# Loads, products and stores of three side jobs cut into quarters and moved to other steps of a two-branch attention kernel

## The chip, the cores and the metric

The kernel runs on one core of a Trainium2 chip. Its engines are TensorE (PE; its weight loads are listed apart as PEld), VectorE (DVE), ScalarE (ACT), GpSimd (POOL) and SyncE (SP), which here only issues DMA transfers. The metric is the device time of one execution in microseconds, lower is better. Three executions of the kernel before gave 2044.47, 2052.12 and 2060.83 us; the time before is their median, 2052.12.

## The reference

Two attention branches over the same input of 2048 tokens and 512 features, with 32 heads of width 16, mixed by a gate per token:

```
qkv = (x @ wqkv)                                  # branch A: softmax attention over all 2048 keys
p = softmax(q k^T * scale);  a = (p v) @ wo

for s in range(4):                                # branch B: four segments of 512 tokens
    p = softmax(qs ks^T * scale + mask); a_dot = p vs        # attention within the segment
    a_mem = (phi(qs) M) / (phi(qs) z + 1e-6)                 # read the memory
    o = g * a_mem + (1 - g) * a_dot
    M, z = M + phi(ks)^T vs, z + sum(phi(ks))                # write the memory
b = o @ wo
out = sigmoid(x . gate_w) * a + (1 - sigmoid(x . gate_w)) * b
```

All matrices are float32. The kernel splits an operand into a high and a low part of the fast matmul type where it needs the accuracy.

## The kernel before

**Stages.** First (0 to about 340 us) projections: queries, keys and values of both branches are computed and put into DRAM, with the memory's numerators (`numd`) and denominators (`dend`) for segments c = 1 to 3. Then comes one long loop over steps, and at the end the last output tiles.

**Steps.** The list `steps` (lines 103 to 109) has two parts. Branch A has 8 groups of 4 heads, each with 4 chunks of 512 queries; such a unit (group, chunk) has 16 steps, one for each block of 128 keys, so 512 steps (`nA`). Branch B has 32 units of 4 steps. In step t, `score_parts` (line 579) computes scores with the keys on the partitions, ACT turns them into p (line 582), in B POOL masks p (line 584), and `values` (line 601) multiplies p of an earlier step with the values, 17 rows for each head, the 17th being the sum of p.

**The rows of maxima.** The score matmuls use 50 rows: 48 of query parts and 2 rows with the negative maximum of each query, so that the exponent is safe. These maxima are computed 22 steps ahead of the scores in A (`max_parts`, matmul at line 197, DVE reduction at line 199). After a unit's last part `finish_max` (lines 158 to 170) reduces on DVE (line 162) and casts on POOL (lines 168, 169); 3 steps later `transpose_max` transposes on PE (line 175), copies on ACT (line 177), and sends two DMA transfers of 8 KB into rows 48 and 49 of the query tile (line 179, `qA<-mt`). In A this is recorded at the end of step 12 of every 16, and the scores of the unit it belongs to begin at step 0 of the next 16.

**Order.** The order is written by hand: `at(t, f)` records work that is issued at the start of step t (`beside`), ahead of the step's own matmuls; the rows of maxima are recorded at its end (`run_late`). Each engine and the SP queue work through their own instructions in this order, and wait for what each instruction needs. SP is not tied to the steps of the other engines: it issues the next transfer as soon as its own waits are met. Each transfer has one of eight semaphores in turn, so it also waits for the transfer that had the same one before.

**The side jobs.** Three of them are touched by the change:
- *Octets.* When the two groups of an octet of 8 heads are done, `a_invert_load` brings the sums of p, `recip` and `invert` make the reciprocal times the gate and store it (`rdA`, line 632), `a_load` (lines 651 to 653) loads the outputs of all 2048 queries and the inverse, broadcast over 16 rows, 1 MB each; `a_mul` scales a quarter on POOL (line 656), and `a_store` (line 658) puts it into DRAM in four transfers. For octet o this begins at t0 = 128 (o + 1) + 4; the load is at t0 + 8, the products at t0 + 13 to t0 + 19, the stores at t0 + 21. Octet 3 falls into branch B.
- *The memory's part.* The same for the numerators of segment c (`m_invert_load` to `m_store`, lines 663 to 679), from t0 = 24 c on: 1 MB of numerators in one transfer, the inverse in four of 256 KB, four products on POOL (line 676), one store of 1 MB.
- *Values.* `load_v` (lines 549 to 557) loads the values of a group of A in four transfers of 136 KB, all at step 64 g - 12.

Other transfers that stand in the same queue are those of the queries (`load_q`, lines 137, 138), the keys (`load_k`, lines 146, 147) and the attention outputs (line 611). POOL also splits the output weights (lines 541, 542), at steps 45 to 51 and 75 to 81.

## Time and profile before

| | us |
|---|---|
| runs (median) | 2044.47, 2052.12, 2060.83 (2052.12) |
| the profiled execution | 2040.8, span 2039.1 |
| PE busy | 2001.6 (98% of the span) |
| DVE busy | 1688.3 (83%) |
| ACT busy | 1478.2 (72%) |
| POOL busy | 212.0 (10%) |
| mean granted TensorE clock | 0.953 |

A page of the profile shows one execution. Busy time is the time in which an engine works on an instruction; a busy PE is not a PE at its peak, since its matmuls overlap. The granted clock is the share of full speed that TensorE is given. "SPq" is the queue of transfers that SP issues: the length of such a line is the time of issuing, not that of moving the data. In a line of the timeline the bracket at its end has the idle time before it and who ended it. The stages by time: projections to about 340 us, branch A's steps from there to about 1590 us, branch B's to about 1965 us, the last output tiles to 2039 us.

### The profile page before, as it was taken

The numbers are of one execution on the slowest core, as the hardware profiler recorded it, in microseconds if no ns is written. First come the engines' busy times: TensorE is split into PE (matmuls) and PEld (weight loads), VectorE is DVE, ScalarE is ACT, GpSimd is POOL, SyncE is SP. The second block draws the span as 40 slices with busy tenths as digits, with TensorE's granted clock in tenths as the row PEclk, the third lists the DMA queues.
The fourth block names the chain that finished last, engine by engine and source line by source line (L and its number), as shares of the span: only waits on it lengthen the run. The fifth ranks groups of instructions, "written<-read, shape, count | busy, mean of one in ns | idle before, by whom it ended". The sixth has DMA issues, their size and how long they took to land.

```text
span 2039.1 us, 41498 instructions
## 1 busy us (share of the span) xinstructions
PE 2001.6 (98%) x16113; PEld 912.9 (45%) x16113; DVE 1688.3 (83%) x3476; ACT 1478.2 (72%) x2823; POOL 212.0 (10%) x372
## 2 busy tenths in 40 slices
PE   8999999999999999999999999999999999999998
PEld 6887665333333333333333333333333344454545
DVE  3235896999999899999999999999998567787842
ACT  3234334888888788888888888888888855565652
POOL 3000000021200100000010000010000023343330
PEclk9999999999999899999999999999999955698989
DMA  6667434032400410110221111130103144546542
GB/s 225 216 232 241 166 141 150 31 100 94 138 15 26 93 44 26 38 35 26 59 66 39 30 30 38 32 94 15 38 15 75 54 121 138 150 146 180 163 132 91
DMA packets 94725, 190.69 MB, mean 94 GB/s; under 512 B 15888, under 2 KB 30000, under 8 KB 91712
## 3 DMA queue, kind: packets, MB, share of 16 engines
q1 hardware_dynamic: 93536, 187.30, 30.6%
q8 instruction: 127, 2.08, 0.4%
q0 software_dynamic: 992, 0.74, 0.2%
q14 instruction: 70, 0.57, 0.1%
HBM read 111.94 MB, written 74.86 MB: 92 GB/s over the span
## 4 chain that ended last, share of the span: by engine, by line
PE 86%; DVE 5%; DMA 4%; ACT 3%; issue 1%; SPq 1%; DVEq 0%; ACTq 0%
PE st L579 35%; PE ops L601 31%; PE pr L274 12%; PE fin L747 4%; DVE pm L199 3%; PE sm L197 2%; ACT p L582 2%; PE sm L210 2%; DMA qA<-mt 1%; ACT oraw L608 1%; DVE sm L215 1%; PE num L422 1%; DMA inv<-rdB 1%; PE mt_ps L175 1%; SPq L694 0%
## 5 line engine op out<-in xcount | busy, mean ns | idle before, releaser
L582 ACT ACTIVATE p<-st 128x512 f32<-128x512 f32 (+2 forms) x2432 | 1298.2, 585 | 301.0 <-PE sm L210 120.8
L199 DVE TENSOR_REDUCE pm<-sm 128x1 f32<-128x512 f32 x2048 | 1254.5, 684 | 31.2 <-PE sm L197 25.1
L579 PE MATMUL st<-qA,k 50*128 50x512 f32 x2048 | 751.4, 447 | 7.7 <-DMA qA<-mt 4.8
L197 PE MATMUL sm<-k,qA 48*128 48x512 f32 x2048 | 751.6, 451 | 0.7 <-DVE pm L199 0.5
L601 PE MATMUL ops<-p,vA 128*17 128x256 f32 x8176 | 645.5, 388 | 5.7 <-ACT oraw L608 5.6
L579 PEld LDWEIGHTS st<-qA,k 50*128 50x128 f32 x2048 | 303.4, 185 | 433.2 <-ACT p L582 411.2
L215 DVE CUSTOM_DVE_ANT_0 sm<-sm,cmask 128x256 f32<-128x256 f32 (+3 forms) x512 | 244.0, 512 | 104.7 <-PE sm L210 81.4
L197 PEld LDWEIGHTS sm<-k,qA 48*128 48x128 f32 x2048 | 310.6, 185 | 24.9 <-DVE pm L199 12.4
L601 PEld LDWEIGHTS ops<-p,vA 128*17 128x17 f32 x8176 | 135.7, 95 | 367.6 <-issue 347.4
L210 PE MATMUL sm<-k,qB 48*128 48x256 f32 (+3 forms) x512 | 183.7, 446 | 5.3 <-DVE pm L215 2.8
L579 PE MATMUL st<-qB,k 50*128 50x256 f32 (+3 forms) x512 | 174.0, 441 | 0.8 <-ACT p L582 0.2
L579 PEld LDWEIGHTS st<-qB,k 50*128 50x128 f32 x512 | 100.4, 235 | 133.5 <-issue 63.1
L168 POOL CAST ms<-nm 128x16 fp32r<-128x16 f32 x64 | 14.1, 220 | 1200.3 <-DVE nm L162 1150.0
L601 PE MATMUL ops<-p,vB 128*17 128x512 f32 (+3 forms) x1024 | 121.6, 556 | 0.0
L323 DVE TENSOR_TENSOR q<-pr,q 128x512 fp32r<-128x512 f32 x64 | 44.0, 687 | 88.0 <-ACT q L316 84.7
L210 PEld LDWEIGHTS sm<-k,qB 48*128 48x128 f32 x512 | 101.8, 233 | 14.7 <-DVE pm L215 9.8
L584 POOL TENSOR_SCALAR_AFFINE_SELECT p<-p 128x512 f32<-128x512 f32 x128 | 82.8, 647 | 244.2 <-ACT p L582 244.2
L316 ACT CAST q<-pr 128x512 fp32r<-128x512 f32 x64 | 37.4, 585 | 82.8 <-PE pr L274 65.6
L215 DVE DVE_READ_ACCUMULATOR2_ANT pm<- 128x1 f32 x512 | 72.2, 141 | 0.1
L274 PE MATMUL pr<-xh,wql 128*128 128x512 f32 x128 | 55.5, 434 | 8.0 <-ACT xh L367 6.0
L274 PE MATMUL pr<-xl,wqh 128*128 128x512 f32 x128 | 51.5, 402 | 0.0
L274 PE MATMUL pr<-xh,wqh 128*128 128x512 f32 x128 | 51.2, 400 | 0.0
(137 smaller groups left out, 1258.4 us busy)
## 6 DMA issues: line engine op xcount, KB each, us to landing
qdA<-q SPq DMA_DIRECT2D x32, 256.0 KB
kdA<-q SPq DMA_DIRECT2D x32, 256.0 KB
qdB<-q SPq DMA_DIRECT2D x32, 256.0 KB
k<-kdA SPq DMA_DIRECT2D x64, 128.0 KB
kdB<-q SPq DMA_DIRECT2D x32, 256.0 KB
qA<-qdA SPq DMA_DIRECT2D x64, 128.0 KB
odA<-oraw SPq DMA_DIRECT2D x32, 256.0 KB
k<-kdB SPq DMA_DIRECT2D x64, 128.0 KB
```

The lines of the kernel that those rows point to most:

```text
L197: nc.tensor.matmul(ps, rows(q[:, :, s * 128:(s + 1) * 128], h, 48), rows(kt_[side, g, kc], h, 48), start=True, stop=True)
L199: nc.vector.tensor_reduce(pm[:, h, s, kc:kc + 1], ps, axis=AX.X, op=ALU.max)
L210: nc.tensor.matmul(ps[:, n0:n0 + n], rows(q[:, :, s * 128:(s + 1) * 128], h, 48), rows(kt_[side, g, c][:, :, :n], h, 48), start=True, stop ...
L215: nc.vector.tensor_tensor_reduce(r, r, cmask[:, CH - n:], 1.0, -3.0e38, ALU.add, ALU.max, pm[:, h - per + 1 + e, s, 0:1])
L274: nc.tensor.matmul(ps, l(a, k), r(b, k), start=(n == 0), stop=(n == 11))
L316: nc.scalar.copy(q1, ps)
L323: nc.vector.tensor_sub(q2, ps, q1.bitcast(F32))
L579: nc.tensor.matmul(ps[:, h % per, :n], rows(k[:, :, b * 128:(b + 1) * 128], h, 50), rows(q[:, :, q0:], h, 50), start=True, stop=True)
L582: nc.scalar.activation(p[:, h - per + 1:h + 1, :n], ps[:, :, :n], AF.Exp, scale=SCALE)
L584: nc.gpsimd.affine_select(out=p[:, :, 0:128], in_=p[:, :, 0:128], pattern=[[0, 4], [1, 128]], base=0, channel_multiplier=-1, compare_op=AL ...
L601: nc.tensor.matmul(ops[32 * h:32 * h + 17, q0 + a:q0 + b], v[h], p[:, h, a:b], start=(i == 0 and a == 0), stop=(i == last and b == n), til ...
L747: nc.tensor.matmul(ps, l[:, o], r[:, o], start=(n == 0), stop=(n == 23))
```

## The change

The three side jobs are cut into quarters, each with its own load, product and store. A new helper, `apart(t, n)`, picks n steps from t on that are at least 3 apart and whose number modulo 16 is 0 to 8 or 14. A quarter's product is recorded 4 steps after its load, its store 6 steps after it. For octet 3 the quarters are 2 steps apart instead.

```diff
-    def load_v(side, i):
+    def load_v(side, i, c=0):
         if side == "A":
-            t = va.tile([128, 4, 4, 68], F32, tag="v", name=f"vA{i}")
-            for c in range(NCH):
-                nc.sync.dma_start(t[:, c], vdA[c][i])
+            t = vt[side, i] if c else va.tile([128, 4, 4, 68], F32, tag="v", name=f"vA{i}")
+            nc.sync.dma_start(t[:, c], vdA[c][i])
...
-    def a_load(o):
-        nc.sync.dma_start(big(("Ar", o), "raw"), odA[o][:, 0:16].rearrange("h r t -> r h t"))
-        nc.sync.dma_start(big(("Ai", o), "inv"), heads(rdA[o], S))
+    def a_load(o, c):
+        if c == 0:
+            big(("Ar", o), "raw")
+            big(("Ai", o), "inv")
+        ts = slice(c * CH, c * CH + CH)
+        nc.sync.dma_start(held["Ar", o][:, c], odA[o][:, 0:16, ts].rearrange("h r t -> r h t"))
+        nc.sync.dma_start(held["Ai", o][:, c], heads(rdA[o][:, ts], CH))
...
-    def a_store(o):
-        for c in range(NCH):
-            nc.sync.dma_start(atd[c][:, o], held["Ar", o][:, c])
+    def a_store(o, c):
+        nc.sync.dma_start(atd[c][:, o], held["Ar", o][:, c])
...
-    def m_load(c):
-        nc.sync.dma_start(big(("Mr", c), "am"), numd[c])
-        t = big(("Mi", c), "at")
-        for o in range(NO):
-            nc.sync.dma_start(t[:, o], heads(rdM[c][8 * o:8 * o + 8], CH))
+    def m_load(c, o):
+        if o == 0:
+            big(("Mr", c), "am")
+            big(("Mi", c), "at")
+        nc.sync.dma_start(held["Mr", c][:, o], numd[c][:, o])
+        nc.sync.dma_start(held["Mi", c][:, o], heads(rdM[c][8 * o:8 * o + 8], CH))
...
-    def m_store(c):
-        nc.sync.dma_start(amd[c], held["Mr", c])
+    def m_store(c, o):
+        nc.sync.dma_start(amd[c][:, o], held["Mr", c][:, o])
...
+    def apart(t, n):
+
+        r = []
+        while len(r) < n:
+            if t % 16 in (0, 1, 2, 3, 4, 5, 6, 7, 8, 14):
+                r.append(t)
+                t += 3
+            else:
+                t += 1
+        return r
+
     for g in range(NG):
-        at(max(0, g * 64 - 12), lambda g=g: load_v("A", g))
+        for c in range(NCH):
+            at(max(0, g * 64 - 18 + 2 * c), lambda g=g, c=c: load_v("A", g, c))
...
-        at(t0 + 7, lambda c=c: m_load(c))
-        for o in range(NO):
-            at(t0 + 10 + 2 * o, lambda c=c, o=o: m_mul(c, o))
-        at(t0 + 18, lambda c=c: m_store(c))
+        for o, n in enumerate(apart(t0 + 8, NO)):
+            at(n, lambda c=c, o=o: m_load(c, o))
+            at(n + 4, lambda c=c, o=o: m_mul(c, o))
+            at(n + 6, lambda c=c, o=o: m_store(c, o))
...
-        at(t0 + 8, lambda o=o: a_load(o))
-        for c in range(NCH):
-            at(t0 + 13 + 2 * c, lambda o=o, c=c: a_mul(o, c))
-        at(t0 + 21, lambda o=o: a_store(o))
+        for c, n in enumerate(apart(t0 + 9, NCH) if o < NO - 1 else range(t0 + 9, t0 + 9 + 2 * NCH, 2)):
+            at(n, lambda o=o, c=c: a_load(o, c))
+            at(n + 4, lambda o=o, c=c: a_mul(o, c))
+            at(n + 6, lambda o=o, c=c: a_store(o, c))
```

For octets 0 to 2 the loads so come at t0 + 10, 13, 16 and 19 (steps 142, 145, 148 and 151 for octet 0), the products at 146, 149, 152 and 155, the stores at 148, 151, 154 and 157. For the memory's part the loads are at steps 32, 35, 38, 46 (c = 1), 56, 62, 65, 68 (c = 2) and 80, 83, 86, 94 (c = 3). The values of group g come at 64 g - 18, - 16, - 14 and - 12. The values of branch B are loaded as before.

## The prediction

> **What bounds the kernel now.** I read the waits first, then the DMA queue's timeline around the longest of them, the engines' timeline there, and the windows of 10 us. The wait that carries this case is one line: engine, who waited for what, us in total, times, longest.

> ```profile
> PE st L579 <- DMA qA<-mt: 4.8, 3, 2.0
> ```

> TensorE waits three times for a row of maxima, the 16 KB that line 179 sends into the query tile. Over the page's 40 slices of 51 us one slice of the long stage shows it: DVE and the granted clock fall together in the 14th.

> ```profile
> DVE  3235896999999899999999999999998567787842
> ...
> PEclk9999999999999899999999999999999955698989
> ```

> From 350 to 1590 us (attention over all keys, 512 steps in 32 units of 16) PE and DVE are both busy 98 to 100%, so what stops PE there is lost for good. In the B stage after it, DVE is 5 to 9 tenths busy and the clock wanders between 0.50 and 1.00. The timeline of the DMA queue (start, length of the issue) shows the cause of the first wait:

> ```profile
> 651.91 1.28 SPq L179 DMA_DIRECT2D qA<-mt  x2
> ...
> 687.97 0.34 SPq L632 DMA_DIRECT2D rdA<-rec  x1
> 688.35 0.59 SPq L652 DMA_DIRECT2D raw<-odA  x1
> 689.52 0.54 SPq L653 DMA_DIRECT2D inv<-rdA  x1
> 692.59 1.41 SPq L179 DMA_DIRECT2D qA<-mt  x2
> 694.10 0.34 SPq L146 DMA_DIRECT2D k<-kdA  x1
> ...
> 738.44 1.30 SPq L179 DMA_DIRECT2D qA<-mt  x2
> 778.07 1.28 SPq L179 DMA_DIRECT2D qA<-mt  x2
> ```

> Two loads of 1 MB (L652, L653) go out 3 to 4 us ahead of the row. At the 210 GB/s of the window 690 to 700, 2.1 MB take 10 us, to about 698.5, and the chain of waits has the row landing 8.87 us after its issue. Its first reader should have run at 699.6:

> ```profile
> 701.59 0.46 PE L579 MATMUL st<-qA,k 50*128 50x512 f32 x1 [2.00 <-DMA qA<-mt]
> ...
> 702.60 4.96 POOL L656 TENSOR_TENSOR raw<-raw,inv 128x512 f32<-128x512 f32 x4 [17.21 <-DMA inv<-rdA]
> ...
> 702.81 0.79 PE L579 MATMUL st<-qA,k 50*128 50x512 f32 x1
> ```

> After the gap the same matmul takes 0.79 us where it took 0.50. Windows (PE, PEld, DVE, ACT, POOL busy; then clock, DMA share, GB/s):

> ```profile
> 690.00:700.00 10.00, 9.59 (x97) 3.32 (x93) 9.96 (x17) 8.83 (x17) 0.00 (x0) 1.00 0.96 210
> 700.00:710.00 10.00, 8.41 (x52) 2.93 (x52) 5.31 (x9) 4.93 (x9) 4.96 (x4) 0.64 0.19 32
> 710.00:720.00 10.00, 10.00 (x88) 3.26 (x84) 8.71 (x15) 7.66 (x15) 0.00 (x0) 0.85 0.73 210
> ...
> 1020.00:1030.00 10.00, 8.85 (x94) 3.10 (x86) 8.88 (x16) 7.85 (x16) 4.99 (x4) 1.00 0.54 110
> 1340.00:1350.00 10.00, 8.37 (x86) 2.96 (x84) 8.40 (x15) 7.42 (x14) 4.99 (x4) 1.00 0.48 98
> ```

> Only the first gap cost clock; the second and third (waits of 1.15 and 1.63 us) stayed at 1.00.

> **The change, part by part.** The price of each stall is read from the distance between two rows of maxima. Undisturbed it is 39.63 us (778.07 - 738.44). The three units after a load of an octet take 45.85, 40.85 (from 1016.92 to 1057.77) and 41.34 us (from 1336.27 to 1377.61): 6.22 + 1.22 + 1.71 = 9.15 us over. The units before them take 40.68, but that 1.05 is the reciprocals (four of 0.34 and a product of 0.29 on a full DVE), which stay.

> *Octets 0 to 2.* The row is queued at the end of the octet's step t0 + 8 (step 140 for octet 0). The old loads are recorded at the start of that step, ahead of it; the first new quarter comes at step 142, behind it. SP runs ahead of the steps as far as its waits let it, so quarter 0 (2 x 256 KB), the 384 KB of a key tile and quarter 1 will leave together right behind the row, some 1.4 MB; only quarters 2 and 3 are held, by the attention output's wait for ACT (L611) and the stores' wait for POOL. What counts is therefore the place behind the row, not the three steps between. Removed: 9.15 us.

> The next row (step 156) has the store of quarter 2 ahead of it in the queue. That store waits for its product, recorded at step 152, ahead of the cast of the maxima (step 153) on POOL. Quarter 2 is issued behind L611, 12.7 us after the row (664.61 after 651.91), and before the cast some 20 us remain; 2 MB took at most 14.3 us from issue to product (688.35 to 702.60). Cost 0; without that cover the cast itself would be late, and with it the row. The store of quarter 3 is behind the row.

> *Octet 3 (B stage).* Loads at 525, 527, 529, 531 instead of all at 524; the products keep steps 529 to 535 among POOL's masks of p, which the values' matmuls wait for. The 2 MB filled the DMA from 1660 to 1670 (share 1.01), yet the units around it take 12.34 and 12.33 us with or without: nothing to gain. Quarter 3 now waits for the store of quarter 0 and thus for a product: issue about 1681, 11 us before its product began (1692.14). A quarter needs 2.5 us at 210 GB/s plus a fixed part that I bound between 1.55 us (a landing of 64 KB, rdM<-rec) and 5.7 us (inv<-rdB in the chain). 4 to 8 us: cost 0.

> *The memory's part.* Chunks c = 1 to 3, loads of 256 KB and four stores in place of one. Rows in this stretch are 39.9 to 40.5 us apart, 2.57 us over in total, where three sets of reciprocals at 1.05 would give 3.15: no stall to remove. Stores of quarters 1 and 2 of c = 1 come ahead of the row of step 44; their products wait only for POOL's cast at 445.1, so they leave by about 447, five us before that row (452.03). Two products fall among POOL's splits of the output weights (0.61 + 1.28 us each), with over 25 us to the next cast. Cost 0, at most one late row: 1.2 to 6.2 us.

> *Values.* The same 32 loads of 136 KB; two of each four now leave right behind a row, two stay behind L611. No wait for them is in the list. 0.

> *Issue.* Octets gain 4 x 6 loads, the memory's part 3 x 3 loads and 3 x 3 stores: 42 issues of 0.34 to 0.6 us, some 19 us of a queue that waits 645.7 us for rows of maxima alone. 0.

> [...]

> Sum: 9.15 us less. The profiled execution took 2040.8 (span 2039.1), so it would take 2031.7. The median shown is 2052.12, 11.3 above it; the same saving from the median gives **2043.0**.

> **The rivals.**
> *Only the waits come back.* The gap and the fall of the clock may be neighbours rather than cause and effect: then 2.00 + 1.15 + 1.63 = 4.8 us return and the other 4.4 us stay, 2047.3. Against it: the clock fell within 1.3 us after the gap and nowhere else between 350 and 1620. For it: two like gaps cost none.
> [...]

> *The clock falls at all three gaps in the runs that set the median.* 3 x 6.22 = 18.7 us, 2033.5. For it: the profiled run is 11.3 below the median, and two more falls of some 4.5 each are 9.

> *A row is held up by what follows it too.* 1.4 MB right behind it instead of 2 MB ahead; if the transfers share the engines rather than follow one another, the row is late as before: no gain, 2052. Against: at 694.10 and in every fourth unit 384 KB follow a row at once, and from 612 us on no unit without an octet is longer than 39.65.

> *Slower: the half clock in B lasts longer.* Everything after 1580 shifts by 9 us, and B stands at the edge: half clock from 1626 to 1720, 0.84 to 1750, 1.00 from 1780. Units take 12.33 us at half clock against 10.35, 9.89 and 10.20 at 0.84; with output products 13.8 against 11.4 (mean of the five from 1785.20 to 1842.15). If it stayed half until 1842: 3 x 2.2 + 5 x 2.4 = 18.6 us more, net 9.4 slower, 2061.5. It decides from some 40 us of 0.84 clock lost on. For it: the runs differ by 16 us without any change. Against: nothing in the change makes PE wait there.

> **How the numbers follow.** Forecast 0.56; only the waits 0.12; three falls 0.10; no gain 0.10; half clock 0.12. The range: the forecast less the 7.7 by which the lowest run lies under the median, and on to the three falls with some of the same, 2031; above, past no gain and into the half clock, 2056. What a measurement of this kernel can tell from no change is about 1%, 20.5 us. Faster by that, under 2031.6, is the lower part of the three falls and the tail of the forecast: 0.13. Over 2072.6 is only the worst of the half clock: 0.07. Same: 0.80.

> **What would show it.** Rows of maxima 39.6 us apart in the units after octets 0 to 2 (40.7 in those with reciprocals), no line "PE st <- DMA qA<-mt", clock 1.00 from 700 to 720, loads of an octet issued behind the row. Wrong would be: a row still landing over 7 us after its issue, POOL's cast of the maxima behind a product that waits for its quarter, or B longer than its old 458 us (1581 to 2039) by more than 9.

## The result and the profile after

| | before | after |
|---|---|---|
| first comparison, median (range, runs) | 2050.55 (2044.47 to 2060.83, 4) | 2027.20 (2026.33 to 2030.35, 4) |
| profiled execution (span) | 2040.8 (2039.1) | 2026.4 (2024.7) |
| mean granted clock | 0.953 | 0.96 |

The ratio of after to before is 0.9884, with a 95% interval of 0.9842 to 0.9926. Two later comparisons, with 12 runs of the changed kernel each, give 0.9937 (0.9911 to 0.9963) and 0.9931 (0.9904 to 0.9957): 0.6 to 0.7% faster, some 13 to 14 us. The first comparison flatters the change, since its four runs of the kernel before were high: their median is 2050.55, and the later batches have 2042.30 to 2046.91.

In the list of waits of the changed kernel no line has a score matmul waiting for `qA<-mt`. The 14th slice of the page, where DVE and the granted clock both had an 8, is filled. (The clock's 8 in the 7th slice is the half clock up to 354 us; it lies ahead of the stretch that the change works on.)

```profile
DVE  4235886999999999999999999999998576687842
...
PEclk9999998999999999999999999999999965599999
```

The timeline of the DMA queue (start, length of the issue, line, transfer) shows the row of maxima of 694.67 with octet 0's loads (now L655, L656) behind it:

```profile
690.06 0.34 SPq L631 DMA_DIRECT2D rdA<-rec  x1
694.67 1.32 SPq L179 DMA_DIRECT2D qA<-mt  x2
696.04 0.57 SPq L655 DMA_DIRECT2D raw<-odA  x1
696.72 0.57 SPq L656 DMA_DIRECT2D inv<-rdA  x1
697.38 0.53 SPq L146 DMA_DIRECT2D k<-kdA  x1
...
699.35 0.52 SPq L655 DMA_DIRECT2D raw<-odA  x1
699.91 0.60 SPq L656 DMA_DIRECT2D inv<-rdA  x1
707.37 0.34 SPq L610 DMA_DIRECT2D odA<-oraw  x1
...
708.25 0.53 SPq L655 DMA_DIRECT2D raw<-odA  x1
...
712.27 0.54 SPq L655 DMA_DIRECT2D raw<-odA  x1
...
734.30 1.41 SPq L179 DMA_DIRECT2D qA<-mt  x2
735.81 0.35 SPq L662 DMA_DIRECT2D atd<-raw  x1
```

Quarter 0, the key tile and quarter 1 go out within 6 us of the row; quarter 2 waits until the attention output of 707.37 has been issued. The next row, 734.30, comes 39.63 us after this one. The windows at the places of the three old gaps (busy time of PE, PEld, DVE, ACT, POOL with counts; clock, DMA share, GB/s) are full, and the clock stays at 1.00:

```profile
700.00:710.00 10.00, 9.81 (x100) 3.44 (x96) 9.80 (x17) 9.05 (x18) 2.57 (x2) 1.00 0.61 132
710.00:720.00 10.00, 10.00 (x104) 3.44 (x96) 10.00 (x17) 8.93 (x18) 1.28 (x1) 1.00 0.92 238
1020.00:1030.00 10.00, 9.81 (x98) 3.43 (x97) 9.80 (x17) 9.05 (x18) 1.56 (x2) 1.00 0.49 150
1340.00:1350.00 10.00, 9.81 (x104) 3.44 (x96) 9.80 (x17) 9.05 (x18) 1.29 (x1) 1.00 0.57 135
```

POOL's timeline shows that the products (L659) leave the cast of the next maxima (L168) alone: quarter 2 is done by 715.10, and the cast comes at 727.35 as soon as DVE has finished; the fourth product stands right behind it.

```profile
713.82 1.28 POOL L659 TENSOR_TENSOR raw<-raw,inv 128x512 f32<-128x512 f32 x1 [6.95 <-DMA inv<-rdA]
727.35 0.20 POOL L168 CAST ms<-nm 128x16 fp32r<-128x16 f32 x1 [12.25 <-DVE nm L162]
...
727.81 1.28 POOL L659 TENSOR_TENSOR raw<-raw,inv 128x512 f32<-128x512 f32 x1
```

To see where time goes, I cut each profiled span at two places of the DMA queue: the first row of branch A after 350 us and the last one. "A" is the stretch between them, "rest" what follows (branch A's last 50 us or so, branch B and the end; branch A's last scores come at 1621 us in the kernel before, not at the 1590 of the stages by time). Between the profiles of before and after A went from 1198.80 to 1189.55, 9.25 us less; rest from 468.4 to 461.1, 7.3 less; and the projections ahead of A took 2.1 more. So of the 14.4 us between the two spans only 9.25 stand where the change works.

### The profile page after: what moved, and what is told of

It reads as the page before. It is cut to its first block, busy times and chain, and to the rows that moved or that the text cites. A ratio compares the mean times of both kernels' runs of the same rounds, so it can differ in the third digit from the quotient of the medians.

```text
span 2024.7 us, 41583 instructions
## 1 busy us (share of the span) xinstructions
PE 1991.4 (98%) x16113; PEld 909.2 (45%) x16113; DVE 1687.3 (83%) x3476; ACT 1478.6 (73%) x2823; POOL 212.9 (11%) x372
## 4 chain that ended last, share of the span: by engine, by line
PE 88%; DVE 4%; ACT 3%; DMA 3%; issue 1%; SPq 1%; POOL 0%; DVEq 0%; ACTq 0%
PE st L578 36%; PE ops L600 32%; PE pr L274 11%; PE fin L750 4%; PE sm L197 2%; PE sm L210 2%; ACT p L581 2%; DVE pm L199 1%; ACT oraw L607 1%; DMA raw<-xT 1%; DVE sm L215 1%; PE num L422 1%; PE mt_ps L175 1%; DMA at<-atd 1%; DMA k<-kdB 0%
## 5 line engine op out<-in xcount | busy, mean ns | idle before, releaser
L168 POOL CAST ms<-nm 128x16 fp32r<-128x16 f32 x64 | 14.1, 220 | 1112.6 <-DVE nm L162 1062.3
L600 PE MATMUL ops<-p,vB 128*17 128x512 f32 (+3 forms) x1024 | 117.1, 538 | 0.3 <-ACT oraw L607 0.3
```

The lines of the kernel that those rows point to most:

```text
L600: nc.tensor.matmul(ops[32 * h:32 * h + 17, q0 + a:q0 + b], v[h], p[:, h, a:b], start=(i == 0 and a == 0), stop=(i == last and b == n), til ...
```

## The experiments

Each batch of kernels ran on one chip beside runs of the kernel before. This table gathers what was read from their profiles. The waits are those of PE for the row. An octet's unit means here the one after its loads.

| kernel | A, us | waits after octets 0, 1, 2 | rest, us | ratio to before (95%) |
|---|---|---|---|---|
| before | 1198.80 | 2.00, 1.15, 1.63 | 468.4 | |
| before_again | 1205.10 | 0.95, 2.34, 2.26 | 465.5 | 1.0020 (0.9993 to 1.0047) |
| rest_only | 1200.78 | 1.42, 1.89, 2.27 | 466.1 | 1.0009 (0.9986 to 1.0031) |
| three_ahead | 1220.14 | 5.79, 6.50, 6.39 | 469.0 | 1.0102 (1.0042 to 1.0162) |
| quarters_ahead | 1201.19 | 0.58, 1.28, 1.29 | 458.1 | 0.9931 (0.9902 to 0.9960) |
| quarters_again | 1197.06 | none, 1.50, 1.73 | 465.3 | 0.9957 (0.9934 to 0.9980) |
| after | 1189.55 | none | 461.1 | 0.9884 (0.9842 to 0.9926) |
| after_again | 1189.59 | none | 470.3 | 0.9937 (0.9911 to 0.9963) |
| after_third | 1189.48 | none | 462.1 | 0.9931 (0.9904 to 0.9957) |
| octets_only | 1189.58 | none | 476.5 | 0.9936 (0.9905 to 0.9968) |
| whole_behind | 1189.57 | none | 464.2 | 0.9950 (0.9924 to 0.9976) |
| half_ahead | 1189.34 | none | 464.8 | 0.9941 (0.9908 to 0.9974) |
| octet3_whole | 1189.62 | none | 468.0 | 0.9936 (0.9913 to 0.9960) |
| recip_one | 1188.18 | none | 460.4 | 0.9922 (0.9890 to 0.9954) |

**The kernel before, once more (before_again).** The same kernel, profiled a second time.

> The kernel before, unchanged, for a second profile and for its spread. Theory one (the surplus of the saving over 9.15 us comes from the clock falling at more of the three gaps than in the first profile): two or three of the units after octets 0 to 2 are longer than 45 us, and the part of the loop over all keys is 4 to 9 us longer than the first profile's 1198.80 us between its first and last row of maxima. Theory two (it comes from stage B): those units again take 45.9, 40.9 and 41.3 us, and the rest of the execution after the last row of branch A takes more than the first profile's 468.4 us.

The median was 2048.14 of 12 runs (2030.6 to 2056.5), against 2042.57 of the 30 runs of the kernel before on that chip (2030.58 to 2056.15). The profile has the three waits again, with other lengths and other consequences. Its three first readers, from PE's timeline (in the bracket the idle time before), and the windows behind the second and third:

```profile
704.69 0.47 PE L579 MATMUL st<-qA,k 50*128 50x512 f32 x1 [0.95 <-DMA qA<-mt]
...
1025.20 0.46 PE L579 MATMUL st<-qA,k 50*128 50x512 f32 x1 [2.34 <-DMA qA<-mt]
...
1351.22 0.74 PE L579 MATMUL st<-qA,k 50*128 50x512 f32 x1 [2.26 <-DMA qA<-mt]
```

```profile
700.00:710.00 10.00, 9.05 (x92) 3.33 (x88) 9.09 (x16) 8.05 (x16) 3.84 (x4) 1.00 0.53 110
1020.00:1030.00 10.00, 7.66 (x68) 2.43 (x60) 7.00 (x12) 6.16 (x12) 4.98 (x4) 0.85 0.55 104
1030.00:1040.00 10.00, 10.00 (x60) 3.19 (x60) 5.77 (x10) 5.33 (x11) 0.00 (x0) 0.50 0.54 181
1350.00:1360.00 10.00, 8.78 (x50) 2.89 (x52) 5.16 (x8) 4.45 (x9) 4.97 (x4) 0.56 0.09 16
```

Here the first gap left the clock at 1.00, and after the second and third it was halved: after the second, PE ran a whole window at 0.50, with 60 matmuls where a full one has about 100. The three units were 40.64, 47.62 and 46.10 us long, 15.5 us over instead of 9.2. This is the first of the two theories: two units over 45 us and A 6.3 us longer. The rest, 465.5 us, is no longer than the first profile's 468.4, as the second would have it. The saving that the change can bring thus differs from execution to execution; the last section has what was measured of the falls.

**The parts by themselves (octets_only, rest_only).** One kernel has only the octets' part of the change, the other only the memory's part and the values:

```diff
# octets_only, against the changed kernel
...
-            at(max(0, g * 64 - 18 + 2 * c), lambda g=g, c=c: load_v("A", g, c))
+            at(max(0, g * 64 - 12), lambda g=g, c=c: load_v("A", g, c))
...
-        for o, n in enumerate(apart(t0 + 8, NO)):
-            at(n, lambda c=c, o=o: m_load(c, o))
-            at(n + 4, lambda c=c, o=o: m_mul(c, o))
-            at(n + 6, lambda c=c, o=o: m_store(c, o))
+        at(t0 + 7, lambda c=c: m_load(c))
+        for o in range(NO):
+            at(t0 + 10 + 2 * o, lambda c=c, o=o: m_mul(c, o))
+        at(t0 + 18, lambda c=c: m_store(c))
# rest_only, against the changed kernel
...
-        for c, n in enumerate(apart(t0 + 9, NCH) if o < NO - 1 else range(t0 + 9, t0 + 9 + 2 * NCH, 2)):
-            at(n, lambda o=o, c=c: a_load(o, c))
-            at(n + 4, lambda o=o, c=c: a_mul(o, c))
-            at(n + 6, lambda o=o, c=c: a_store(o, c))
+        at(t0 + 8, lambda o=o: a_load(o))
+        for c in range(NCH):
+            at(t0 + 13 + 2 * c, lambda o=o, c=c: a_mul(o, c))
+        at(t0 + 21, lambda o=o: a_store(o))
```

> Only the octets in quarters; the memory's part and the values as in the kernel before. Both theories on the clock: within 3 us of the changed kernel (2027), ratio to before 0.985 to 0.992, every row of maxima 39.63 or 40.68 us after the last from 612 us on. Rival that the memory's part or the values carry part of the saving: 2030 to 2040.

> Only the memory's part and the values in quarters; the octets as in the kernel before. My reading: no change, ratio 0.997 to 1.003, the wait of the score matmul for the row of maxima is still there three times. Rival that they carry part of the saving: ratio 0.992 to 0.996.

Medians were 2030.88 (octets_only, 10 runs) and 2044.96 (rest_only, 12 runs) against 2042.57. A is 1189.58 with the octets' part alone, the same as with all of the change, and 1200.78 with all but it, with the three waits of the kernel before. So the octets carry the whole gain; the memory's part and the values, with their 18 more issues, give and cost nothing that can be measured. The ratio of octets_only, 0.9936, is above the 0.985 to 0.992 that was expected, and so is that of whole_behind below, 0.9950: both expectations leaned on the first comparison's 0.9884. Their A, the same as the changed kernel's to 0.03 us, is as expected.

**Place or size (whole_behind, half_ahead, quarters_ahead, quarters_again).** The change moves an octet's loads behind the row and cuts them to quarters. Two kernels leave the loads whole: the first moves both behind the row, the second only the inverse.

```diff
# whole_behind, against the kernel before
-        at(t0 + 8, lambda o=o: a_load(o))
+        late_by = 2 if o < NO - 1 else 0
+        at(t0 + 8 + late_by, lambda o=o: a_load(o))
...
-            at(t0 + 13 + 2 * c, lambda o=o, c=c: a_mul(o, c))
-        at(t0 + 21, lambda o=o: a_store(o))
+            at(t0 + 13 + late_by + 2 * c, lambda o=o, c=c: a_mul(o, c))
+        at(t0 + 21 + late_by, lambda o=o: a_store(o))
# half_ahead, against whole_behind
+        at(t0 + 8, lambda o=o: a_load_raw(o))
         at(t0 + 8 + late_by, lambda o=o: a_load(o))
```

In half_ahead `a_load_raw` has the load of the outputs, and `a_load` keeps that of the inverse.

> The kernel before with the two whole loads of 1 MB of octets 0 to 2, their products and stores two steps later, so that the loads are queued behind the row of maxima instead of ahead of it; nothing is cut into quarters. If the place in the queue is all: the time of the changed kernel, 2027, ratio 0.985 to 0.992, no wait for the row. If the cutting matters (2 MB behind a row hold it up too, or hold the keys and queries behind them): the wait stays or another takes its place, 2035 to 2050.

> Whole loads, the outputs' 1 MB ahead of the row and the inverse's 1 MB behind it. If a row lands when what is ahead of it in the queue has landed: 1 MB less at 210 GB/s is 5 us earlier, more than the longest wait of 2.3, so no wait and 1189.6 us in branch A. If any large transfer ahead holds it up: a wait stays.

Medians were 2030.52 (9 runs, before 2042.57) and 2029.21 (8 runs, before 2043.19). Both have no wait for a row, and A at 1189.57 and 1189.34. The DMA queue's timeline, first of whole_behind, then of half_ahead:

```profile
690.69 0.34 SPq L632 DMA_DIRECT2D rdA<-rec  x1
695.30 1.31 SPq L179 DMA_DIRECT2D qA<-mt  x2
696.66 0.58 SPq L652 DMA_DIRECT2D raw<-odA  x1
697.34 0.57 SPq L653 DMA_DIRECT2D inv<-rdA  x1
```

```profile
688.11 0.59 SPq L652 DMA_DIRECT2D raw<-odA  x1
692.34 1.36 SPq L179 DMA_DIRECT2D qA<-mt  x2
693.81 0.58 SPq L655 DMA_DIRECT2D inv<-rdA  x1
```

Two whole loads right behind the row cost nothing, and one of 1 MB four microseconds ahead of it costs nothing either. The DMA packets of the traces show it directly. A row is 32 packets of 512 bytes, and the last of them ended 2.2 us after the row's issue at the three octets of whole_behind and of the changed kernel, which is also the median of all rows of the kernel before (2.17). With two whole loads ahead (before, before_again, rest_only) it ended 6.9 to 8.1 us after the issue, in half_ahead 2.3 to 2.8. So what is queued behind does not hold the row up, and a load of 1 MB four microseconds ahead holds it up by 0.7 us at most. Cutting is not needed.

The other two runs, of one and the same kernel in two batches, cut the loads and leave all eight ahead of the row. The products are two steps apart there, from t0 + 13 on, and the stores too, from t0 + 15 on, so they also differ a little from both other kernels:

```diff
# quarters_ahead and quarters_again, against the changed kernel
-        for c, n in enumerate(apart(t0 + 9, NCH) if o < NO - 1 else range(t0 + 9, t0 + 9 + 2 * NCH, 2)):
-            at(n, lambda o=o, c=c: a_load(o, c))
+        for c in range(NCH):
+            n = t0 + 9 + 2 * c
+            at(t0 + 8 if o < NO - 1 else n, lambda o=o, c=c: a_load(o, c))
```

> The changed kernel with all four quarters of octets 0 to 2 queued ahead of the row of maxima (step t0 + 8), products and stores two steps apart. If the place is all: the three waits of 1 to 2.3 us are back, branch A's steps take 1198 to 1206 us, and the time is that of the kernel before. If it is the size of a transfer that holds the row up: no wait, 1189.6 us.

> The eight quarter loads of octets 0 to 2 ahead of the row of maxima again, beside the changed kernel on the same chip, because the first such run had the waits of the kernel before and yet the time of the changed kernel. If the place alone counts: three waits for the row again, branch A at 1195 to 1205 us against 1189.6, and a median 5 to 12 us above the changed kernel's of the same chip. If the size of the pieces counts as much (waits of 1.3 us or less, too short to cost the clock in most executions): waits of 0.3 to 1.3 us with at most one fall of the clock, branch A at 1191 to 1196 us, and a median 1 to 4 us above the changed kernel's.

> The changed kernel, unchanged, with more runs. If its saving is the three gaps and what the clock loses after them, the ratio is that of the two kernels that only moved or cut the octets' loads: 0.993 to 0.996, about 12 us, and the first figure of 0.9884 was a few runs that lay well on both sides. If the memory's part or the values add something of their own: 0.986 to 0.990. Branch A's steps take 1189.6 us between the first and the last row of maxima, as in its first profile.

> The changed kernel, as the measure for the run beside it: rows of maxima 39.6 us apart after octets 0 to 2, branch A at 1189.6 us, no wait for a row, 0.992 to 0.995 of the kernel before.

The first of these was a miss. The waits were back (0.58 to 1.29 us, where 1 to 2.3 were expected) and A was 1201.19, as the place in the queue asks, yet the median was 2030.46 of 10 runs, beside 2028.63 of 12 of the changed kernel in the same batch (after_again; before 2043.19). The second was run because of it: A 1197.06, median 2037.78 beside 2029.70 (after_third), 12 runs each, before 2046.91. By A and by the 8.1 us between the medians this one came as the place alone would have it, though with two waits and not three. Both batches stand on record under the same chip number. Over both, the quarters ahead of the row have a median of 2034.6 from 22 runs, the changed kernel one of 2029.4 from 24, and the kernel before lies 14.6 and 17.2 us above the latter in the two batches. Both ratios of the quarters to the kernel before have intervals below 1. So the quarters alone bring part of the gain and the place the rest. How much each is, these runs leave open: by the medians two thirds are the quarters', by A (1199.1 as the mean of the two profiles, 1201.6 as that of the three with the old loads, 1189.5) a fifth.

Why quarters hold the row up less can be read from the timeline of quarters_ahead:

```profile
688.54 0.58 SPq L655 DMA_DIRECT2D raw<-odA  x1
...
692.22 1.37 SPq L656 DMA_DIRECT2D inv<-rdA  x1
...
694.28 0.60 SPq L656 DMA_DIRECT2D inv<-rdA  x1
694.98 1.41 SPq L179 DMA_DIRECT2D qA<-mt  x2
```

and from its windows of 2 us, ahead of which I put the same ones of the kernel before:

```profile
694.00:696.00 2.00, 2.00 (x24) 0.71 (x24) 2.00 (x5) 1.86 (x4) 0.00 (x0) 1.00 1.18 250
...
698.00:700.00 2.00, 1.59 (x20) 0.43 (x12) 2.00 (x4) 1.79 (x4) 0.00 (x0) 1.00 0.95 192
700.00:702.00 2.00, 0.41 (x4) 0.33 (x4) 0.15 (x1) 0.00 (x0) 0.00 (x0) 1.00 0.88 142
```

```profile
694.00:696.00 2.00, 2.00 (x24) 0.56 (x20) 2.00 (x4) 1.73 (x5) 0.46 (x1) 1.00 1.01 307
...
698.00:700.00 2.00, 1.78 (x21) 0.49 (x20) 2.00 (x4) 1.87 (x4) 1.27 (x1) 1.00 0.91 186
700.00:702.00 2.00, 1.64 (x16) 0.76 (x16) 1.45 (x3) 1.19 (x3) 1.29 (x1) 1.00 0.11 33
```

The eight issues push the row itself back: the unit before it takes 42.88 us, and 40.68 in the kernel before. But the 2 MB move faster (307 GB/s against 250 in the window from 694), and after 700 little is left of them (33 GB/s), where two whole loads still moved 142 GB/s until 702. The row's last packet ended 3.8 to 6.4 us after its issue at the six places of the two runs, against 6.9 to 8.1. PE waits 0.58 us here instead of 2.00. Waits of 0 to 1.73 us in place of 0.95 to 2.34 cost less. The clock fell at 3 of these 6 places (waits of 1.28, 1.29 and 1.73 us) and at five of the nine with whole loads, which is no clear difference. For these sizes, 256 KB against 1 MB, the smaller loads have no price in these windows, nor in the times: whole_behind and octets_only, with 6 and 24 loads at octets 0 to 2 and ratios of 0.9950 and 0.9936, differ by less than their intervals.

**A third load ahead (three_ahead).** The kernel before, with one more load of 1 MB ahead of the row at octets 0 to 2, into a tile that nothing reads:

```diff
     def a_load(o):
...
+        if o < NO - 1:
+            spare = fr.tile([128, NO, CH], F32, tag="am", name="spare")
+            nc.sync.dma_start(spare, odA[o][:, 0:16].rearrange("h r t -> r h t"))
```

> The kernel before with a third load of 1 MB (the outputs once more, into a tile that nothing reads) ahead of the row for octets 0 to 2. Each row lands 5 us later, each gap is 6 to 7.5 us. If the clock falls because of the gap: it falls at all three, the units after the octets are 10 to 13 us over 39.63, branch A's steps take 1219 to 1229 us. If the falls have another cause and only meet a gap by chance: 6 to 7.5 us over at most of them, 1207 to 1213 us.

Its line in the list of waits, and the windows behind the first gap:

```profile
PE st L579 <- DMA qA<-mt: 18.7, 3, 6.5
```

```profile
700.00:710.00 10.00, 4.21 (x32) 1.58 (x28) 3.12 (x6) 2.55 (x5) 4.93 (x4) 0.79 0.78 163
710.00:720.00 10.00, 10.00 (x60) 3.05 (x60) 6.44 (x10) 6.02 (x11) 0.00 (x0) 0.52 0.19 60
```

The waits grew from a mean of 1.77 us (nine of them in the three profiles with the old loads) to 6.23: 4.46 us for 1.05 MB, which would be 235 GB/s, within the 192 to 250 GB/s that the windows of the kernel before show while its loads move. The row's last packet ended 11.8 to 12.5 us after its issue, against 6.9 to 8.1 with two loads ahead. So here the row waits for about as long as the bytes ahead of it take. The clock fell at all three, A was 1220.14 as expected (though the third unit was 9.00 us over, where 10 to 13 were), and the median of two runs was 2064.52 against 2043.19.

**Octet 3 whole (octet3_whole).** The changed kernel, with octet 3 loaded whole at t0 + 8 and its four stores at t0 + 21, as before:

```diff
+        if o == NO - 1:
+            at(t0 + 8, lambda o=o: a_load_whole(o))
...
-            at(n + 6, lambda o=o, c=c: a_store(o, c))
+            at(n + 6 if o < NO - 1 else t0 + 21, lambda o=o, c=c: a_store(o, c))
```

> The changed kernel with octet 3, the one in branch B, loaded whole at step 524 and stored at 537 as in the kernel before. My reading: the rows of maxima of B are sent so far ahead that their place does not matter, so nothing changes: ratio to before 0.991 to 0.996 as for the changed kernel. Rival that octet 3's quarters shorten or lengthen B: 4 us or more to either side, under 0.990 or over 0.997.

The median was 2032.18 (12 runs, before 2042.30 of 18), its ratio that of the changed kernel elsewhere. Octet 3's quarters neither gain nor cost anything that can be measured.

**One reciprocal instead of four (recip_one).** An attempt to go on from the changed kernel: the four reciprocals of a set become one, and the gate's product goes from DVE to POOL (octet 3's stays on DVE).

```diff
-            nc.vector.tensor_mul(t, t, gate)
+            (nc.gpsimd if key[0] == "M" or key[1] < NO - 1 else nc.vector).tensor_mul(t, t, gate)
...
-        for i in range(4):
-            at(t0 + 3 + i, lambda c=c, i=i: recip(("M", c), i))
+        at(t0 + 5, lambda c=c: recip(("M", c), 0, 1))
...
-        for i in range(4):
-            at(t0 + 4 + i, lambda o=o, i=i: recip(("A", o), i))
+        at(t0 + 6, lambda o=o: recip(("A", o), 0, 1))
```

> An attempt at a faster version on top of the changed kernel: each job of branch A makes its reciprocals in one instruction of 128x128 (0.95 us in the profile) instead of four of 128x32 (0.34 us each), and POOL instead of DVE multiplies with the gate (0.29 us on DVE). DVE is full there, and a unit with the four is 1.05 us longer than one without. Expected: 0.71 us less on DVE for each of six jobs, units of 40.0 instead of 40.68 after the octets, branch A's steps 1185.5 to 1187.5 us instead of 1189.6, 2 to 4 us less in all. If a single pause of DVE of 0.95 us costs as much as four short ones, nothing changes: 1189 to 1190 us.

The units with reciprocals went from 40.68 to 40.45 us and A to 1188.18, 1.4 us less than the changed kernel's. That lies between the two forecasts, 1185.5 to 1187.5 and 1189 to 1190. The four took 4 x 0.34 = 1.36 us on DVE and the one 0.94, so with the product of 0.29 DVE had some 0.7 us less to do for each set, as expected; but the unit became only 0.23 shorter. Why the rest does not come back was not tried. The median of 2027.35 (7 runs) is the lowest of the batches, but its ratio of 0.9922 cannot be told from the changed kernel's.

## Why the prediction was right and wrong

*What bounds the kernel, and the mechanism: right.* The place of the octets' loads ahead of the row made PE wait. octets_only has the gain and rest_only has none of it; whole_behind and half_ahead have it with whole loads; three_ahead enlarges the wait by about the time of one more load. The rival by which a row is held up by what follows it too is ruled out by the packets: 2.2 us from issue to the last one, with 2 MB right behind or without.

*"What counts is therefore the place behind the row, not the three steps between": right for the trace, too narrow for the time.* The place is enough (whole_behind). But quarters ahead of the row also bring part of the gain; in the one place whose windows are shown they move faster. The prediction gave the cutting no effect of its own.

*What would show it:* rows 39.62 to 39.64 us apart after octets 0 to 2, no wait for a row, clock 1.00 from 700 to 720, loads behind the row, quarter 2 held by the attention output and issued 13.6 us after the row (12.7 forecast), the cast of the maxima on time. All of it came.

*Octet 3, memory's part, values, 42 more issues at 0: right.* Bounds are the ratios of octet3_whole (0.9936) and rest_only (1.0009, 0.9986 to 1.0031). Octet 3's last quarter left at 1666.24 in the profile after, earlier than the 1681 of the prediction.

*"Removed: 9.15 us": right for that one execution, too small for the kernel.* Between the two profiles A lost 9.25 us. But the price came from three gaps of which one had cost the clock. In nine such gaps (before, before_again, rest_only) the clock fell at five; the three profiles stood 9.2, 15.5 and 11.2 us above 1189.6, 12.0 in the mean. The parts agree: a mean wait of 1.77 us, and in five cases of nine a fall that cost 3.9 more, make 4.0 us a gap, and 12 for three. That A's 9.25 agrees with the forecast is no test of the price: both were read from the same profile of the kernel before, and another one would have forecast 15.5 or 11.2. The comparisons of many runs give 12.9 (0.63% of 2043.2) and 14.1 us (0.69% of 2046.9), with about 5 us of uncertainty on either side. This is where two of the rivals lay: "only the waits come back" was wrong, since A lost more than the waits; "the clock falls at all three gaps" was half right, with five of nine.

*"The same saving from the median gives 2043.0": the step that failed, with the saving of 9.15 as the second part of the miss.* The base, 2052.12, was the median of three runs. Batches of 30, 29, 18 and 23 runs of the same kernel have medians of 2042.57, 2043.19, 2042.30 and 2046.91: the base was 5 to 10 us too high. The changed kernel's first 2027.2 is 15.8 us under the forecast and 3.8 under the foot of the range. In the two batches with 12 runs of it, 2028.63 and 2029.70 lie 14.4 and 13.3 under the forecast; 8.9 and 5.2 of that are the base (2052.12 less the batch's own median of the kernel before), and 5.4 and 8.1 the saving that came on top of 9.15 (3.8 and 4.9, if it is taken from the ratios). The profiled execution, at 2040.8, was nearer to the kernel's usual time than the median of three, and the sum against it, 2031.7, is 2.0 to 4.5 us above what was measured. The prediction carried the 11.3 between the two along as it stood. What held those three runs up is not known: they left no profile, and the record does not name the chip of the first comparison. The changed kernel was to be within 1% of the one before with a chance of 0.80: the first comparison, 1.16%, is past that bound, and the two of 12 runs are within it.

*"B longer than its old 458 us by more than 9", and the half clock in B:* did not come. My "rest" starts at the last row of branch A, some 10 us ahead of the 1581 from which the prediction counts B; branch B's first scores come at 1622. In the seven profiles without a wait for a row (recip_one apart) rest is 461.1 to 476.5, with a mean of 466.7; in the four with the old loads ahead of the row, three_ahead among them, it is 465.5 to 469.0, with a mean of 467.3. Branch B neither gains nor loses by the change as far as these show. It only scatters by up to 15 us between executions, and in the first pair of profiles that happened to help by 7.3.

## What to carry to other kernels

A small transfer that an engine waits for should be queued ahead of large ones on its queue: here two loads of 1 MB ahead delayed it by 4.7 to 5.9 us and a third by some 4.5 more, and the same loads behind it cost nothing. Read the price of such a stall from several executions, since a gap of about the same length may cost only itself (waits of 1.63 and 1.89 us here) or also several microseconds of half clock (1.42 and 1.73). And where two or three runs of a kernel differ by 16 us, do not take their median as the base of a forecast whose saving is smaller than that.

## What the runs showed of the hardware

The granted clock fell after shorter waits than the 2.00 us of the first profile. In all profiles, PE waited for a row of maxima 17 times. At the seven waits of 2.0 us or more the clock fell every time; at the ten from 0.58 to 1.89 it fell four times (1.28 and 1.29 in quarters_ahead, 1.42 in rest_only and 1.73 in quarters_again) and stayed six times (0.58, 0.95, 1.15, 1.50, 1.63, 1.89). A fall cost 2.6 to 5.7 us beyond the wait. In branch A's first steps the clock stood at 0.50 until 347.8 us in the profile before and until 353.7 in the one after; from there to branch A's last scores it fell once in the profile before, behind the wait of 2.00 us, and never in the one after.

```profile
1341.10:1344.52 3.42, 2.17 (x24) 0.56 (x20) 2.74 (x5) 2.23 (x5) 0.00 (x0) 1.00 0.99 192
1344.52:1347.93 3.41, 3.02 (x28) 1.19 (x28) 2.48 (x5) 2.23 (x5) 3.33 (x3) 1.00 0.10 24
```

```profile
1339.19:1342.60 3.41, 2.12 (x24) 0.79 (x23) 2.14 (x5) 1.81 (x5) 1.88 (x2) 1.00 0.52 104
1342.60:1346.02 3.42, 3.42 (x24) 1.11 (x24) 2.42 (x4) 1.98 (x4) 0.61 (x1) 0.50 0.01 2
```

So in this stage about the same wait cost only itself (1.63 us) or also a fall (1.29); the two differ in where they lay to these boundaries. In branch B idle time does not part the cases: in the profile before the clock fell at 1726.81 us, after a piece of 3.41 us in which PE was busy for 3.37. What made it fall there these runs do not settle.

Two things stay open: why the same two loads delay the row so differently from place to place that PE waits 0.95 us in one and 2.34 in another; and why the clock stands at 0.50 for so much of the 160 us from 1620 to 1780, in branch B, with and without the change (133 us in before and after, 129 in rest_only, 152 in octets_only, 113 in whole_behind). Neither was tried.
